# Mean of x block 0 from two partial sums, its statistics later; blocks 1 to 3 normalized in halves; z2 weights in 128-row pieces

## The chip, the cores and the metric

The kernel runs on one core of a Trainium2 chip. A core has five engines that run side by side and meet through semaphores: TensorE (PE; its weight loads are listed as PEld), VectorE (DVE), ScalarE (ACT), GpSimd (POOL) and SyncE (SP, which here only issues DMAs). Sixteen DMA engines move data between device memory and the core's on-chip memory; SP, ACT and POOL each have a queue from which DMAs are issued. TensorE writes to eight banks of PSUM, from which ACT and DVE read.

The metric is the device time of one execution in microseconds. Times inside an execution are counted from the start of its profiled span.

## The reference

With x of 2048 rows (tokens) and 512 columns, all in bf16, the result is a sum of three terms:

```python
xn = layernorm(x)                      # over the 512 columns, eps 1e-5
# A: 32 heads of 16, each token attends to itself and 7 tokens 2, 4, ... 14 back
qkv = xn @ wqkv
attn = softmax(einsum(q, k_gathered) / 4)
a = (attn @ v_gathered) @ wo
# B: gated mixer
z  = gelu(xn @ w_in)                   # 512 -> 1792
z1, z2 = z[:, :896], layernorm(z[:, 896:])
g  = w_sp @ z2 + b_sp[:, None]         # 2048 x 2048, over tokens
b  = (z1 * g) @ w_out
out = x + a + b
```

The change concerns the first microseconds: the layernorm of the first four blocks of 128 tokens, and `z2 = gelu(xn @ w_in[:, 896:])` of these blocks.

## The kernel before

The kernel is one straight program without loops at run time. The 2048 tokens are 16 blocks of 128. Every operation is a task with an engine, what it reads and writes, and an estimated duration (`Plan.add`). A planner (`Plan.schedule`, line 95) puts the tasks of each engine in an order by estimated times. `plan.orders` (line 1053) lists, engine by engine, names of tasks that must follow one another as written, and so fixes nearly all of the order around the change. Each engine then runs its tasks strictly in that order, a DMA issue being a task of the queue's engine. A task waits for the semaphores of what it depends on, and all that stands behind it on the engine waits too.

Layernorm of a block is `ln_block` (line 608): on DVE `bnst` (bn_stats, line 612, sums over 512 columns) and `bnag` (bn_aggr, line 615, mean and variance plus epsilon); on POOL `rstd` (line 617, the power -0.5); on DVE `norm` (line 626, subtract the mean and multiply by rstd). For blocks 0 to 3 TensorE transposes the result by multiplying with a unit matrix (`xTr`, line 642, two halves `a` and `b` of two 128 x 128 tiles each), and ACT copies each half from PSUM to the place of the transposed xn (`xTe`, line 648). Blocks from 4 on are transposed by a DMA (line 630).

Block 0 takes a shorter way, since TensorE has no other work yet. Once the mean is known, x is centred in two halves (`ctr1`, `ctr0`, line 621) and transposed without rstd; z2 of this block is computed from the centred x, and rstd is applied as the scale of the gelu that reads PSUM (`z2g0`, line 829). The properly normalized block 0, needed by Q, K, V and z1 later, is made by `norm0` and transposed afterwards in two halves (`xNr0`, `xNr1`, line 661, copied by `xNe`, line 665).

z2 of a block (`z2_block`, line 806) is two halves of 448 columns (`z2_b_0`, `z2_b_1`), each four matmuls (line 818) that add up over the four 128-row chunks of the weights, and a gelu with its sum. For blocks 0 to 3 each half is two tasks of two matmuls, `a` for chunks 0 and 1 and `b` for 2 and 3. The weights of a half come in two loads of 256 rows (`ld_win_h`, line 555): chunks 2 and 3 on the ACT queue, 0 and 1 on SP's. Four such loads (`ldw_in2a_0`, `ldw_in2a_1`, `ldw_in2b_0`, `ldw_in2b_1`) are issued between the loads of x (`ld_x`, line 545).

Until x arrives TensorE multiplies constants (`warm`, 28 matmuls of 146 columns, line 584), and once more ahead of the first real matmul (`fill0`, 320 columns). Behind the z2 matmuls of blocks 0 to 3 come, without a break in TensorE's order, Q and K (line 694) and V (line 676) of these blocks, then the same for the later ones, z1 (line 841), the token mixing g (line 951) and the outputs (lines 1017 and 1021).

The order of DVE and TensorE in the stretch that the change rewrites:

```python
bnst0 bnag0 ctr1 ctr0 bnst1 bnag1 norm0 norm1 bnst2 bnag2 bnst3 norm2 bnag3 bnst4 norm3
warm xTr0b xTr0a fill0 z2_0_0b z2_0_1b z2_0_0a xTr1a xTr1b z2_0_1a xNr0 z2_1_0a z2_1_0b z2_1_1a xTr2a
xTr2b z2_1_1b xNr1 z2_2_0a z2_2_0b xTr3a xTr3b z2_2_1a z2_2_1b z2_3_0a z2_3_0b z2_3_1a z2_3_1b Q0_0 K0_0
```

Of the kernel before, what the change touches and what calls it, by code (L numbers as in the profile page):

```python
# [14 lines left out]
class Plan:  # L15
# [290 lines left out]
ALU = mybir.AluOpType  # L306
# [9 lines left out]
    warm=28,  # L316
    fill0=1,
# [4 lines left out]
def build_kernel(nc, A_x, A_wqkv, A_wo, B_x, B_w_in, B_w_sp, B_b_sp, B_w_out, out, report=False, sched_kw=None,  # L322
                 cfg=None, emit=True):
    cfg = dict(DEFAULT_CFG, **(cfg or {}))
    S = A_x.shape[1]
# [8 lines left out]
    KP = 16  # L334
    FILL = cfg["fill"]
# [57 lines left out]
    for name, n in (("prime", 4), ("Z", 128), ("st6", NB * 9),  # L393
                    ("mv", NB * 2), ("vpe", NB), ("rstd", NB), ("s1", 2 * NB), ("s2", NB), ("m2", NB), ("msq", NB),
                    ("vpe2", NB), ("rstd2", NB), ("mhalf", 4)):
        foff[name] = fb
        fb += n
# [4 lines left out]
    with ExitStack() as es:  # L402
# [30 lines left out]
        def R1(key, name, n, o_=0):  # L433
            R(key, "sb", [(off[name] + o_, off[name] + o_ + n)])
# [42 lines left out]
        R1("xn0", "attn", 512, 1024)  # L477
        for b in range(NB):
            R(("xnT", b), "sb", [(off["xnT"] + dc * S + 128 * b, off["xnT"] + dc * S + 128 * b + 128)
                                 for dc in range(4)])  # L480
            R1(("OT", b), "OT", 512, 512 * b)
            R1(("z2", b), "z2", FH, FH * b)
        for nm, lo, hi, h0, h1 in (("w_in1", 0, FH, 0, 4), (("w_in2a", 0), FH, FH + HF, 0, 2),
                                   (("w_in2a", 1), FH, FH + HF, 2, 4), (("w_in2b", 0), FH + HF, 2 * FH, 0, 2),
                                   (("w_in2b", 1), FH + HF, 2 * FH, 2, 4)):
            R(nm, "sb", [(off["w_in"] + dc * 1792 + lo, off["w_in"] + dc * 1792 + hi) for dc in range(h0, h1)])
# [66 lines left out]
        def ld_win_h(nm, lo, n):  # L553
            for h in range(2):
                dma(("sp", "act")[h], (lambda h: lambda e: e.dma_start(
                    AC(off["w_in"] + lo + 2 * 1792 * h, [[1792, 2], [1, n]]),
                    B_w_in[256 * h: 256 * h + 256, lo: lo + n].rearrange("(c p) n -> p c n", p=128)))(h),
                    256 * n * 2, (nm, h), writes=[(nm, h)], name="ld%s_%d" % (nm, h))
# [3 lines left out]
        ld_win_h("w_in2a", FH, HF)  # L562
        ld_win_h("w_in2b", FH + HF, HF)
        ld_x(2, "act")
        ld_x(3, "sp")
        for which, eng in ((0, "sp"), (1, "sp")):
            dma(eng, (lambda which: lambda e: e.dma_start(
                AC(off["wqk"] + 512 * which, [[1024, 4], [1, 512]]),
                A_wqkv[:, 512 * which: 512 * which + 512].rearrange("(c p) n -> p c n", p=128)))(which),
                512 * 512 * 2, ("wqk", which), reads=[("w_in2b", 1)],  # L570
                writes=[(("wq", "wk")[which], c) for c in range(4)],
                name="ld%s" % ("qk"[which]))
        for b in range(4, min(8, NB)):
            ld_x(b, "sp", after=[("w_in2b", 1)])
# [33 lines left out]
        def ln_block(b):  # L608
# [10 lines left out]
            if b == 0:  # L619
                for h in (1, 0):  # L620
                    T("dve", (lambda h: lambda v: v.tensor_scalar(A("attn", 256, 256 * h), xin[:, 256 * h: 256 * h + 256],  # L621
                                                                  Fv("mv", 1, 2 * b), None, ALU.subtract))(h),
                      reads=[("xin", xs_), ("mv", b)], writes=[("xc", h)], est=250, name="ctr%d" % h)
            xo = off["attn"] + 1024 if b == 0 else off["xn"] + 512 * sl
            xk = "xn0" if b == 0 else ("xn", sl)
            T("dve", lambda v: v.tensor_scalar(AC(xo, [[1, 512]]), xin, Fv("mv", 1, 2 * b),
                                               Fv("rstd", 1, b), ALU.subtract, ALU.mult),
              reads=[("xin", xs_), ("mv", b), ("rstd", b)], writes=[xk], est=400, name="norm%d" % b)
# [6 lines left out]
            src, sk = (off["attn"], lambda h: ("xc", h)) if b == 0 else (xo, lambda h: xk)  # L635
# [19 lines left out]
        def xn0_half(h):  # L655
            k = next_bank()

            def tr(t):
                last = None
                for i in range(2):  # L660
                    last = t.matmul(ps[:, 512 * k + 128 * i: 512 * k + 128 * i + 128],  # L661
                                    A("attn", 128, 1024 + 256 * h + 128 * i), ident, start=True, stop=True)
                return last
            T("pe", tr, reads=["xn0", "ident"], writes=[("ps", k)], est=2 * c_mm(128), name="xNr%d" % h)
            T("act", lambda a: a.activation(AC(off["xnT"] + 2 * h * S, [[S, 2], [1, 128]]),
                                            ps[:, 512 * k: 512 * k + 256].rearrange("p (c n) -> p c n", c=2), ACTF.Copy),
              reads=[("ps", k)], writes=[("xnTh", 0, h)], est=c_act(256) - 30, name="xNe%d" % h)
# [138 lines left out]
        def z2_block(b):  # L806
            for hf in range(2):
# [5 lines left out]
                def mm(t, hs, first, k=k, c0=c0):  # L813
                    last = None
                    for h in hs:
                        for dc in (2 * h, 2 * h + 1):
                            st = AC(off["attn"] + 512 + 128 * dc if b == 0 else off["xnT"] + dc * S + 128 * b, [[1, 128]])
                            last = t.matmul(ps[:, 512 * k: 512 * k + HF], st, AC(off["w_in"] + 1792 * dc + c0, [[1, HF]]),  # L818
                                            start=(h == first and dc == 2 * h), stop=(h != first and dc == 2 * h + 1))
                    return last  # L820
                if b < 4:
                    for n_, h in enumerate((1, 0) if b == 0 else (0, 1)):
                        T("pe", (lambda mm, h: lambda t: mm(t, (h,), 1 if b == 0 else 0))(mm, h),
                          reads=[("xcT", h) if b == 0 else ("xnTh", b, h), (wk_, h)], writes=[("ps", k)], est=2 * c_mm(HF),
                          name="z2_%d_%d%s" % (b, hf, "ab"[h]))
                else:
                    T("pe", (lambda mm: lambda t: mm(t, (0, 1), 0))(mm), reads=[("xnT", b), (wk_, 0), (wk_, 1)],
                      writes=[("ps", k)], est=4 * c_mm(HF), name="z2_%d_%d" % (b, hf))
# [55 lines left out]
        for j in range(NJ):  # L884
# [6 lines left out]
            if j == 0:  # L891
                for fn_, b, k0 in ((ln_block, 0, 3), (xn0_half, 0, 3), (ln_block, 1, 1), (z2_block, 0, 5), (ln_block, 2, 3),
                                   (z2_block, 1, 7), (xn0_half, 1, 5), (ln_block, 3, 5), (z2_block, 2, 1), (z2_block, 3, 3)):
                    ring[0] = k0
                    fn_(b)
                setup_masks()
                ring[0] = 5
            else:
                for b in bl:
                    ln_block(b)  # L900
# [149 lines left out]
        for q in qord:  # L1050
# [4 lines left out]
                bnst0 bnag0 ctr1 ctr0 bnst1 bnag1 norm0 norm1 bnst2 bnag2 bnst3 norm2 bnag3 bnst4 norm3  # L1055
            """.split(),
            """
                actprime ldw_in2a_1 ldw_in2b_1 ldx2 xTe0b xTe0a xTe1a xTe1b xNe0 z2g0_0 z2g0_1 xTe2a xTe2b xNe1 z2g1_0
                xTe3a xTe3b z2g1_1
            """.split(),  # L1060
            """
                ldx0 ldx1 ldw_in2a_0 ldw_in2b_0 ldx3 ldx4 ldx5 ldq ldk ldx6 ldx7 ldwv
            """.split(),
            """
                warm xTr0b xTr0a fill0 z2_0_0b z2_0_1b z2_0_0a xTr1a xTr1b z2_0_1a xNr0 z2_1_0a z2_1_0b z2_1_1a xTr2a
                xTr2b z2_1_1b xNr1 z2_2_0a z2_2_0b xTr3a xTr3b z2_2_1a z2_2_1b z2_3_0a z2_3_0b z2_3_1a z2_3_1b Q0_0 K0_0
                Q0_1 K0_1 Q0_2 K0_2 Q0_3 K0_3 V0 V1 V2 V3 V4 V5 V6 V7 Q1_0 K1_0 Q1_1 K1_1 Q1_2 K1_2 Q1_3 K1_3 z2_4_0
                z2_4_1 z2_5_0 z2_5_1 z2_6_0 z2_6_1 z2_7_0 z2_7_1 V8 V9 V10 V11 Q2_0 K2_0 Q2_1 K2_1 Q2_2 K2_2 Q2_3 K2_3
                z2_8_0 z2_8_1 z2_9_0 z2_9_1 z2_10_0 z2_10_1 z2_11_0 z2_11_1 V12 V13 V14 V15 Q3_0 K3_0 Q3_1 K3_1 Q3_2
                K3_2 Q3_3 K3_3 z2_12_0 z2_12_1 z2_13_0 z2_13_1 z2_14_0 z2_14_1 z2_15_0 z2_15_1 z1_0_0 z1_1_0 z1_2_0  # L1070
                z1_3_0 z1_4_0 z1_5_0 z1_6_0 z1_0_1 z1_1_1 z1_2_1 z1_3_1 z1_4_1 z1_5_1 z1_6_1 z1_0_2 z1_1_2 z1_2_2 z1_3_2
                z1_4_2 z1_5_2 z1_6_2 z1_0_3 z1_1_3 z1_2_3 z1_3_3 z1_4_3 z1_5_3 z1_6_3 g0_0 g1_0 g2_0 g3_0 g4_0 g5_0 g6_0
                g0_1 g1_1 g2_1 g3_1 g4_1 g5_1 g6_1 g0_2 g1_2 out0_0 out2_0 g2_2 g3_2 g4_2 g5_2 out1_0 out3_0 g6_2 out4_0
                out6_0 g0_3 g1_3 out5_0 out7_0 g2_3 g3_3 g4_3 g5_3 g6_3 out8_0 out10_0 out9_0 out11_0 out12_0 out14_0
                out13_0 out15_0 out15_1 out15_2
# [93 lines left out]
```

## Time and profile before

| what | value |
|---|---|
| median of three runs | 235.44 us (235.41 to 235.62) |
| the profiled execution | 235.56 us, its span 233.7 us |
| TensorE matmuls busy | 229.1 us (98%) |
| DVE / ACT / POOL busy | 202.5 / 119.2 / 51.3 us |
| x block 0 landed, first work of DVE on it | 3.13 us |
| first z2 matmul | 5.27 us |
| first Q matmul | 12.97 us |
| end of the last matmul in the chain | 231.44 us |

The profile of an execution gives each instruction with its engine, its start and duration, the source line (L818 is line 818 of the kernel), the tiles it writes and reads, and how long its engine was idle just before it, with what ended that wait. Matmuls are pipelined, so a record's length (0.35 us for 448 columns) is more than the time from one start to the next. The chain that ended last is followed back from the last instruction, at each step to what released it, or to the instruction before it on its engine: it is the list of what set the time.

### The profile page before, as it was taken

The numbers are of one execution on the slowest core, as the hardware profiler recorded it, in microseconds if no ns is written. First come the engines' busy times: TensorE is split into PE (matmuls) and PEld (weight loads), VectorE is DVE, ScalarE is ACT, GpSimd is POOL, SyncE is SP. The second block draws the span as 40 slices with busy tenths as digits, with TensorE's granted clock in tenths as the row PEclk, the third lists the DMA queues.
The fourth block names the chain that finished last, engine by engine and source line by source line (L and its number), as shares of the span: only waits on it lengthen the run. The fifth ranks groups of instructions, "written<-read, shape, count | busy, mean of one in ns | idle before, by whom it ended". The sixth has DMA issues, their size and how long they took to land.

```text
span 233.7 us, 2996 instructions
## 1 busy us (share of the span) xinstructions
PE 229.1 (98%) x1108; PEld 112.6 (48%) x1127; DVE 202.5 (87%) x231; ACT 119.2 (51%) x235; POOL 51.3 (22%) x67
## 2 busy tenths in 40 slices
PE   7999999999999999999999999999999999999996
PEld 6554455554554444444444444444444444444444
DVE  4779979989989989998999999999999999989200
ACT  3898678989988978952021124342232415101442
POOL 4528965680880050001301000010000000000000
DMA  7897850399909999681429999999939694920412
GB/s 230 270 246 172 188 137 3 109 198 334 357 22 175 227 253 242 125 227 57 139 74 282 244 178 262 185 279 306 295 73 267 128 235 122 237 39 7 112 48 67
DMA packets 87166, 41.76 MB, mean 179 GB/s; under 512 B 66272, under 2 KB 86000, under 8 KB 87152
## 3 DMA queue, kind: packets, MB, share of 16 engines
q1 hardware_dynamic: 71072, 23.24, 48.2%
q10 hardware_dynamic: 14640, 14.13, 21.0%
q0 software_dynamic: 1440, 4.21, 5.9%
q8 instruction: 9, 0.15, 0.3%
q14 instruction: 5, 0.04, 0.1%
HBM read 20.05 MB, written 5.26 MB: 108 GB/s over the span
## 4 chain that ended last, share of the span: by engine, by line
PE 96%; DMA 1%; issue 1%; DVE 1%; ACT 0%
PE ps L951 41%; PE ps L694 12%; PE ps L818 11%; PE ps L1021 10%; PE ps L841 10%; PE ps L1017 6%; PE ps L676 6%; DMA arena<-in_A_x_dram 1%; PE ps L642 1%; DVE fpool L612 0%; ACT arena L648 0%; DVE arena L621 0%; ACT arena L1030 0%; PE ps L661 0%; DVE fpool L615 0%
## 5 line engine op out<-in xcount | busy, mean ns | idle before, releaser
L951 PE MATMUL ps<-arena 128*128 128x512 bf16 x440 | 97.1, 379 | 0.4
L951 PEld LDWEIGHTS ps<-arena 128*128 128x128 bf16 x448 | 43.8, 98 | 52.8
L945 ACT ACTIVATE ps<-arena 128x512 f32<-128x512 bf16 x28 | 16.5, 599 | 47.8 <-DVE arena L958 47.1
L976 DVE TENSOR_TENSOR arena<-arena 128x4096 bf16<-128x4096 bf16 x16 | 36.3, 2284 | 0.3
L718 DVE TENSOR_TENSOR arena<-arena 128x4096 bf16<-128x4096 bf16 x16 | 36.1, 2280 | 0.1
L980 DVE TENSOR_TENSOR arena<-arena 128x4096 bf16<-128x4096 bf16 (+1 forms) x16 | 28.0, 1753 | 0.3
L694 PE MATMUL ps<-arena 128*128 128x512 bf16 x127 | 28.1, 379 | 0.1
L723 DVE TENSOR_TENSOR arena<-arena 128x4096 bf16<-128x4096 bf16 x12 | 27.4, 2287 | 0.2
L1021 PE MATMUL ps<-arena 128*128 128x512 bf16 (+2 forms) x123 | 26.8, 355 | 0.2
L818 PE MATMUL ps<-arena 128*128 128x448 bf16 x128 | 25.7, 353 | 0.2 <-ACT arena L648 0.2
L1030 ACT ACTIVATE arena<-ps 128x512 bf16<-128x512 f32 (+2 forms) x17 | 9.6, 562 | 30.3 <-PE ps L1021 30.3
L841 PE MATMUL ps<-arena 128*128 128x512 bf16 x109 | 24.0, 379 | 0.2
L694 PEld LDWEIGHTS ps<-arena 128*128 128x128 bf16 x128 | 14.5, 113 | 13.1
L958 DVE TENSOR_TENSOR arena<-ps,arena 128x512 bf16<-128x512 f32 x28 | 19.1, 681 | 1.3 <-PE ps L951 1.3
L1021 PEld LDWEIGHTS ps<-arena 128*128 128x128 bf16 x126 | 13.6, 113 | 11.0
L702 ACT ACTIVATE arena<-ps 128x1024 bf16<-128x1024 f32 x16 | 16.3, 1020 | 3.4 <-PE ps L694 3.0
L818 PEld LDWEIGHTS ps<-arena 128*128 128x128 bf16 x128 | 12.1, 98 | 11.4 <-ACT arena L648 1.0
L846 ACT ACTIVATE arena<-ps 128x512 bf16<-128x512 f32 x28 | 16.0, 595 | 3.2 <-PE ps L841 2.7
L829 ACT ACTIVATE arena<-ps 128x448 bf16<-128x448 f32 x30 | 16.2, 548 | 2.2 <-issue 0.2
L841 PEld LDWEIGHTS ps<-arena 128*128 128x128 bf16 x112 | 11.0, 98 | 13.1
L1017 PE MATMUL ps<-arena 128*128 128x512 bf16 (+2 forms) x71 | 16.7, 355 | 0.1
L851 ACT ACTIVATE arena<-arena 128x896 bf16<-128x896 bf16 x16 | 15.1, 943 | 0.1
(65 smaller groups left out, 194.7 us busy)
## 6 DMA issues: line engine op xcount, KB each, us to landing
arena<-vscr ACTq DMA_DIRECT2D x8, 1152.0 KB, 9.7
arena<-in_A_x_dram ACTq DMA_DIRECT2D x17, 128.0 KB, 5.8
vscr<-arena POOLq DMA_DIRECT2D x16, 128.0 KB, 2.4
arena<-in_A_x_dram SPq DMA_DIRECT2D x15, 128.0 KB, 2.9
out_dram<-arena ACTq DMA_DIRECT2D x15, 128.0 KB, 1.9
arena<-in_A_wqkv_dram SPq DMA_DIRECT2D x3, 512.0 KB, 5.8
ascr<-arena POOLq DMA_DIRECT2D x4, 256.0 KB, 5.1
arena<-ascr POOLq DMA_DIRECT2D x4, 256.0 KB, 4.3
```

The source lines that it names most:

```text
L694: last = t.matmul(bank(k + which), AC(off["wqk"] + 1024 * dc + col0, [[4, 128]]), AC(off["xnT"] + dc * S + 512 * j, [[1, 512]]), start=(dc ...
L718: T("dve", lambda v: v.tensor_tensor(pbv, qb, kb, ALU.mult), reads=[("QT", c, j), ("KT", c, j), ("KTpad", c, j)], writes=[("pb", s_)], est ...
L723: T("dve", lambda v: v.tensor_tensor(A("pb", 4096, 4096 * a), A("pb", 4096, 4096 * a), A("pb", 4096, 4096 * b), ALU.add), reads=[("pb", b) ...
L818: last = t.matmul(ps[:, 512 * k: 512 * k + HF], st, AC(off["w_in"] + 1792 * dc + c0, [[1, HF]]), start=(h == first and dc == 2 * h), stop= ...
L841: lastm = t.matmul(bank(k), AC(off["w_in"] + 1792 * dc + 128 * fc, [[1, 128]]), AC(off["xnT"] + dc * S + 512 * j, [[1, 512]]), start=(dc = ...
L945: T("act", lambda a: a.activation(bank(k), A("bbc", 512, 512 * tc), ACTF.Copy), reads=["bbc"], writes=[("ps", k)], est=c_act(512), name="g ...
L951: last = t.matmul(bank(k), AC(off["z2"] + FH * sh + 128 * fc, [[1, 128]]), AC(off["wT"] + WSL * r_ + sh * 512, [[1, 512]]), start=False, s ...
L958: T("dve", lambda v: v.tensor_tensor(uv, bank(k), uv, ALU.mult), reads=[("ps", k)], writes=[("z1T", fc, tc)], est=c_dve(512) + 20, name="u ...
L976: T("dve", (lambda iv, tv, av: lambda v: v.tensor_tensor(tv, iv, av, ALU.mult))(iv, tv, av), reads=[("attn", j), ("Ve", par)], writes=[("V ...
L980: T("dve", (lambda n: lambda v: v.tensor_tensor(AC(off["Vs"], [[4096, 2], [1, n]]), AC(off["Vs"], [[4096, 2], [1, n]]), AC(off["Vs"] + n, ...
L1017: t.matmul(po, AC(off["OT"] + 512 * ot_pos(tb) + 128 * cc, [[1, 128]]), AC(off["wo"] + 512 * cc + c0, [[1, n]]), start=False, stop=False, ...
L1021: last = t.matmul(po, AC(off["z1T"] + fc * S + t0, [[ts, 128]]), AC(off["w_out"] + 512 * fc + c0, [[1, n]]), start=False, stop=(fc == FC - ...
```

## The change

Five things change, all within the first 13 us.

1. The mean of block 0 no longer comes from bn_stats and bn_aggr. ACT sums 192 of the 512 columns (`sxA`, an activation with an accumulator), DVE the other 320 (`sxD`, a tensor_scalar with an accumulator), each scaled by -1/512; `ctr1` and `ctr0` add both sums to x. In ACT's order `sxA` stands behind the DMA issues.
2. bn_stats and bn_aggr of block 0 move behind those of block 1 (`bnst0`) and behind norm1 (`bnag0`); `norm0` moves behind bnag3. The transposes of the normalized block 0 become one task of four (`xNr`), with one copy of 512 columns (`xNe`), and move to just before z2 of block 3.
3. norm1, norm2 and norm3 are two instructions of 256 columns each, and each transposed half needs only its own.
4. The z2 weights come in eight loads of 128 rows instead of four of 256, and z2 of block 0 is eight tasks of one matmul. In TensorE's order these alternate between the two halves and with the transposes of block 1. The loads of Q's and K's weights and of x blocks 4 to 7 wait for the last piece on ACT's queue (`w_in2b`, 3).
5. The constant matmuls are 27 instead of 28.

```diff
-    warm=28,
+    warm=27,
@@
-        def ld_win_h(nm, lo, n):
-            for h in range(2):
-                dma(("sp", "act")[h], (lambda h: lambda e: e.dma_start(
-                    AC(off["w_in"] + lo + 2 * 1792 * h, [[1792, 2], [1, n]]),
-                    B_w_in[256 * h: 256 * h + 256, lo: lo + n].rearrange("(c p) n -> p c n", p=128)))(h),
-                    256 * n * 2, (nm, h), writes=[(nm, h)], name="ld%s_%d" % (nm, h))
+        def ld_win_c(nm, lo, n):
+            for c in (2, 3, 0, 1):
+                dma("act" if c > 1 else "sp", (lambda c: lambda e: e.dma_start(
+                    AC(off["w_in"] + lo + 1792 * c, [[1, n]]), B_w_in[128 * c: 128 * c + 128, lo: lo + n]))(c),
+                    128 * n * 2, (nm, c), writes=[(nm, c)], name="ld%s_%d" % (nm, c))
@@
-                512 * 512 * 2, ("wqk", which), reads=[("w_in2b", 1)],
+                512 * 512 * 2, ("wqk", which), reads=[("w_in2b", 3)],
...
-            ld_x(b, "sp", after=[("w_in2b", 1)])
+            ld_x(b, "sp", after=[("w_in2b", 3)])
@@ ln_block
-            if b == 0:
-                for h in (1, 0):
-                    T("dve", (lambda h: lambda v: v.tensor_scalar(A("attn", 256, 256 * h), xin[:, 256 * h: 256 * h + 256],
-                                                                  Fv("mv", 1, 2 * b), None, ALU.subtract))(h),
...
+            if b in (1, 2, 3):
+                for h in range(2):
+                    T("dve", (lambda h: lambda v: v.tensor_scalar(AC(xo + 256 * h, [[1, 256]]), xin[:, 256 * h: 256 * h + 256],
+                                                                  Fv("mv", 1, 2 * b), Fv("rstd", 1, b), ALU.subtract,
+                                                                  ALU.mult))(h),
...
@@
-        def xn0_half(h):
+        def xn0_T(_):
...
-                for i in range(2):
+                for i in range(4):
...
+        def centre():
+            xin = xin_ap(0)
+            T("act", lambda a: a.activation(A("attn", XA, 1536 + 512 - XA), xin[:, 512 - XA: 512], ACTF.Copy, scale=-1.0 / D,
+                                            accum_out=Fv("sxa", 1)),
+              reads=[("xin", 0)], writes=["xja", "sxa"], est=460, name="sxA")
+            T("dve", lambda v: v.tensor_scalar(A("attn", 512 - XA, 1536), xin[:, 0: 512 - XA], -1.0 / D, None, ALU.mult, ALU.add,
+                                               accum_out=Fv("sxd", 1)),
+              reads=[("xin", 0)], writes=["xjd", "sxd"], est=500, name="sxD")
+            for h in (1, 0):
+                T("dve", (lambda h: lambda v: v.tensor_scalar(A("attn", 256, 256 * h), xin[:, 256 * h: 256 * h + 256],
+                                                              Fv("sxa", 1), Fv("sxd", 1), ALU.add, ALU.add))(h),
+                  reads=[("xin", 0), "sxa", "sxd"], writes=[("xc", h)], est=200, name="ctr%d" % h)
@@ z2_block
+                order = (2, 3, 0, 1) if b == 0 else (0, 1, 2, 3)
+                runs = [(2,), (3,), (0,), (1,)] if b == 0 else [(0, 1), (2, 3)] if b < 4 else [(0, 1, 2, 3)]
...
@@ plan.orders (DVE, ACT, SP, PE)
-                bnst0 bnag0 ctr1 ctr0 bnst1 bnag1 norm0 norm1 bnst2 bnag2 bnst3 norm2 bnag3 bnst4 norm3
+                sxD ctr1 ctr0 bnst1 bnag1 bnst0 norm1a norm1b bnag0 bnst2 bnag2 bnst3 norm2a norm2b bnag3 norm0 bnst4
+                norm3a norm3b bnag4 bnst5 norm4 bnag5 bnst6 norm5 bnag6 bnst7 norm6 bnag7
...
-                actprime ldw_in2a_1 ldw_in2b_1 ldx2 xTe0b xTe0a xTe1a xTe1b xNe0 z2g0_0 z2g0_1 xTe2a xTe2b xNe1 z2g1_0
-                xTe3a xTe3b z2g1_1
+                actprime ldw_in2a_2 ldw_in2a_3 ldw_in2b_2 ldw_in2b_3 ldx2 sxA xTe0b xTe0a xTe1a xTe1b z2g0_0 z2g0_1
+                xTe2a xTe2b z2g1_0 z2g1_1 xTe3a xTe3b xNe z2g2_0 z2g2_1 z2g3_0 z2g3_1
...
-                ldx0 ldx1 ldw_in2a_0 ldw_in2b_0 ldx3 ldx4 ldx5 ldq ldk ldx6 ldx7 ldwv
+                ldx0 ldx1 ldw_in2a_0 ldw_in2a_1 ldw_in2b_0 ldw_in2b_1 ldx3 ldx4 ldx5 ldq ldk ldx6 ldx7 ldwv
...
-                warm xTr0b xTr0a fill0 z2_0_0b z2_0_1b z2_0_0a xTr1a xTr1b z2_0_1a xNr0 z2_1_0a z2_1_0b z2_1_1a xTr2a
-                xTr2b z2_1_1b xNr1 z2_2_0a z2_2_0b xTr3a xTr3b z2_2_1a z2_2_1b z2_3_0a z2_3_0b z2_3_1a z2_3_1b Q0_0 K0_0
...
+                warm xTr0b xTr0a fill0 z2_0_0c2 z2_0_0c3 z2_0_1c2 z2_0_0c0 z2_0_1c3 z2_0_0c1 xTr1a z2_0_1c0 xTr1b
+                z2_0_1c1 z2_1_0a z2_1_0b z2_1_1a xTr2a z2_1_1b xTr2b z2_2_0a z2_2_1a z2_2_0b xTr3a xTr3b z2_2_1b xNr
+                z2_3_0a z2_3_0b z2_3_1a z2_3_1b Q0_0 K0_0 Q0_1 K0_1 Q0_2 K0_2 Q0_3 K0_3 V0 V1 V2 V3 V4 V5 V6 V7 Q1_0
...
```

## The prediction

> **What bounds the kernel now.** I read the page's first part first: TensorE is busy for 98% of the span, every other engine less.
>
> ```profile
> PE 229.1 (98%) x1108; PEld 112.6 (48%) x1127; DVE 202.5 (87%) x231; ACT 119.2 (51%) x235; POOL 51.3 (22%) x67
> ```
>
> So time can be won only where TensorE waits or does useless work. Next the chain that ended last, in order of time (start, duration, what): all that is not TensorE lies before 5.27 us and behind 231.44 us.
>
> ```profile
> 0.73 2.38 DMA arena<-in_A_x_dram
> ...
> 3.13 0.71 DVE fpool L612
> ...
> 3.86 0.21 DVE fpool L615
> ...
> 4.09 0.30 DVE arena L621
> ...
> 4.83 0.39 ACT arena L648
> ...
> 5.27 1.31 PE ps L818 x6
> 6.58 0.04 issue
> 6.62 0.40 PE ps L642 x4
> ...
> 10.42 0.22 PE ps L642 x4
> 10.64 2.27 PE ps L818 x12
> 12.91 0.05 issue
> 12.97 6.85 PE ps L694 x31
> ```
>
> Here the reader sees the head: x block 0 lands, bn_stats and bn_aggr give its mean (3.13 to 4.07), it is centred, transposed, copied, and useful matmuls begin at 5.27. From there to the first Q matmul at 12.97 are 7.70 us. The undisturbed prices are in the chain too: 2.27/12 = 0.189 us per 448-column matmul (L818), 0.22/4 = 0.055 us per transpose. The stage has 32 and 16 of them, 6.93 us; 0.77 us are stalls. The timeline of this stretch shows which (start, busy, what, idle before it):
>
> ```profile
> 2.63 3.69 SPq L545 DMA_DIRECT2D arena<-in_A_x_dram  x3
> ...
> 5.48 0.63 POOL L617 TENSOR_TENSOR fpool<-fpool 128x1 f32<-128x1 f32 x1 [0.66 <-DVE fpool L615]
> ...
> 6.15 0.41 DVE L626 TENSOR_SCALAR arena<-arena,fpool 128x512 bf16<-128x512 bf16 x1 [0.46 <-POOL fpool L617]
> ...
> 6.62 0.23 PEld L642 LDWEIGHTS ps<-arena 128*128 128x128 bf16 x4 [0.48 <-DVE arena L626]
> ...
> 8.06 0.41 DVE L626 TENSOR_SCALAR arena<-arena,fpool 128x512 bf16<-128x512 bf16 x1
> ...
> 9.48 0.11 PEld L818 LDWEIGHTS ps<-arena 128*128 128x128 bf16 x2 [0.17 <-ACT arena L648]
> ```
>
> TensorE waits at 6.62 for norm1, which waited for POOL's rstd1; at 8.62 for norm2; at 9.48 for a copy on ACT. The head of the stage is thus set by one DVE/POOL chain from ctr1 (4.09) on. The x and weight loads are the other input:
>
> ```profile
> DMA to landing us min/median/max: 2.9/4.1/4.4
> ```
>
> That is the four weight loads (L555). The completion records of the trace put them at 3.74, 5.49, 5.67 and 6.55 us, in order of issue and at some 370 GB/s together with the x loads between them.
>
> **The change, part by part.** The sums are made against the profiled execution: span 233.72, its time 235.56, so 1.84 us around the span; the median of the runs, 235.44, is 0.12 lower. I subtract the gain from the median.
>
> *Mean of block 0.* Before, ctr1 starts 0.96 us behind bn_stats (3.13 to 4.09). Now it waits for two sums.
> - sxD on DVE (320 columns and an accumulator): not in the trace. From below, the plain TENSOR_SCALAR of 256 columns, 0.288 (no accumulator); from above, bn_stats with all 512 columns, 0.69, and an accumulator read as ACT's, 0.20: 0.89. It is nearest to bn_stats, which reduces too: L621 and L626 (0.28 and 0.41 for 256 and 512 columns) show a fixed part of 0.15, so 0.15 + 0.54 x 320/512 = 0.49. It ends at 3.13 + 0.49 = 3.62 (3.42 to 4.02).
> - sxA on ACT (192 columns): an L829 of 448 columns takes 0.64 from its start to the end of its accumulator read (11.11 to 11.75); less 256 columns at (565 - 384)/192 = 0.94 ns, 0.40. But ACT stands in order behind its DMA issues, now five instead of three. Three took 0.87 to 2.34, 0.49 each; five end at 3.32. It runs 3.33 to 3.73.
> - ctr1 then starts at 3.77 (0.035 us for a wait, as between DVE's steps) instead of 4.09: 0.32 earlier, set by ACT. Bounds: 3.63 if the issues cost ACT nothing, 4.06 if sxD takes 0.89.
>
> *DVE and POOL behind it.* From ctr1 to norm1 the trace has 2.06 us (4.09 to 6.15): two centrings, bnst1, bnag1, rstd1. The moved bnst0 (0.69) lies in DVE's 0.46 us wait for POOL and the place that norm0 (0.37) had. rstd1 is now POOL's first power; the first one before took 0.68, the second 0.63, so +0.05. norm1a starts at 3.77 + 2.06 + 0.05 = 5.88. The halves start 0.20 apart (as L621's two), last 0.285, so TensorE may transpose from 5.88 + 0.285 + 0.08 = 6.25 instead of 6.62.
> Behind it come norm1b (0.20), bnag0 (0.11), bnst2 (0.72), bnag2 (0.20) and POOL (0.08 + 0.55): norm2a starts at 7.97 and ends at 8.25; before, norm2 ended at 8.47. rstd0 is done by about 7.2, when ACT first needs it for a gelu. norm0, 0.41, goes ahead of bnst4 and norm3a; norm3a ends near 9.75, as norm3 did (9.71), and xTr3a is not before 10.1: covered.
>
> *TensorE.* One filler matmul less (0.12) ends the fillers at 4.15; the first transpose comes 0.43 behind ctr1, at 4.20: nothing on the path. Matmuls of z2_0 start 1.18 behind ctr1 (5.27 - 4.09): 4.95. In the new order: six matmuls to 6.08; xTr1a waits for norm1a, 6.25; then 1c0, xTr1b, 1c1 to 6.85. z2_1_0a needs xTe1a (0.055 + 0.22 + 0.38 + 0.08 behind xTr1a, in the trace 6.62 to 7.38): 6.99. Six matmuls, 8.12; xTr2a waits for norm2a: 8.33, against 8.62. Left from there: 18 matmuls and 12 transposes, 3.40 + 0.66 = 4.06, and a wait of 0.13 for xTe2a ahead of z2_2_0a (it comes 0.73 behind xTr2a, the work between takes 0.60). Q0 begins at 8.33 + 4.06 + 0.13 + 0.05 = 12.57, against 12.97: **0.40 us earlier**.
>
> *Weights in 128-row pieces.* Bytes are equal; four issues more, two on SP, two on ACT. The trace moves one load after the other at about 365 GB/s, so in order of issue the pieces land at 3.4, 4.1, 4.4, 4.7, 5.0, 5.4, 5.7 and 6.4 (the last, with x2 ahead of it), each with up to 0.7 us of one late queue (2b_1: fifteen of sixteen by 4.75, the last 5.49). Needed at 4.95 to 6.66; where one is 0.3 late, xTr2a's wait for norm2a (0.21) takes most. Bounds: 0 to 0.3 lost; I take 0, as xTr2a hides it. On SP, x3 moves from 2.63 to 3.6 and x4 waits for the last ACT piece instead of 2b_1. The wait before ended at 5.51; now at 5.4 to 5.9. Q's and K's weights, behind it, landed at 11.18 and 12.66; at worst 0.4 later, 13.06, ahead of K0_0 at 12.57 + 0.86 = 13.43. x6 has the same delay, and DVE waits for it (13.05): prod0_0 a bit later, with 1.07 us of DVE idle at 31 us to take it.
>
> *xNr and xNe in one.* Four transposes as before; one 512-column copy (0.60, as L846) for two of 0.40: ACT 0.2 less. Hidden.
>
> *Behind 12.97* TensorE never waits (0.05 us pieces of issue alone), and DVE itself waits for TensorE at 120.9, 170.5 and 205.5, so the gain should run through. The last transposed OT lands at 221.2, about 5 us ahead of its use. Sum: 235.44 - 0.40 = 235.04; I say 235.05. Own range: the ctr1 bounds move it by +0.29 and -0.14, late pieces by +0.3, a faster rstd1 by -0.1: 234.75 to 235.4.
>
> **Rivals.** Changes within 0.2% (0.47 us, 234.97 to 235.91) are about what a measurement cannot tell from none.
> 1. *ACT's five issues hold the mean (slower).* Place: sxA. The longest load issue on a queue near here is 0.69 (L575). Five such end at 0.87 + 5 x 0.69 = 4.32, sxA at 4.72, ctr1 at 4.76: 0.67 late, the chain behind it as computed with -0.40 + 0.99: 236.0. It loses once ctr1 passes 4.17. Against: the three issues before took 0.43, 0.48, 0.49.
> 2. *The clock.* 28 fillers of 146 columns take 3.5 us, 0.83 ns a column; L818 has 0.42. The pace thus doubled between 4.0 and 4.5, 3.4 us behind the first filler, though the granted-clock column says 1.00 throughout. If 27 fillers don't bring it about, and another 3.4 us must pass, until 7.6, z2_0 and xTr1 (half pace 3.46 us from 5.2) end at 8.13 instead of 6.85, xTr2a starts at 9.27 instead of 8.33: 235.04 + 0.9 = 235.95. Against: fillers still reach 4.15, and the last filler before (its record is 0.27, not 0.33) suggests a change near 4.15.
>    [...]
> 3. *Pieces land late (no change).* If small loads ran slower or the queue straggled by another 0.7, the last piece lands past 6.66 + 0.35 and each later tenth is lost; with the longest landing before (4.4 from an issue at 3.06) it is 7.46, so 0.45 lost: 235.5. Against: 128 KB x loads between 224 KB ones did not lower the rate.
>    [...]
> 4. *The stalls close as well.* If ACT issues in no time (ctr1 3.63) and rstd takes 0.55, xTr2a comes 0.25 earlier and the 0.13 wait shrinks: 234.65.
>
> **How the numbers follow.** Forecast 0.60, rival 1 0.10, rival 2 0.08, rival 3 0.13, rival 4 0.09. The forecast's own range has somewhat under half below 234.97 (0.25), the rest within 0.2%. Faster: 0.25 + 0.09 = 0.34. Slower: rival 2, most of rival 1, a corner of rival 3: 0.17. Same: 0.49. The range 234.6 to 235.7 leaves out rival 2 and the upper part of rival 1, about 0.17.
>
> **What would show it.** Right: ctr1 near 3.77 with ACT's sum as releaser, z2 from 4.95, xTr2a held by norm2a near 8.3, Q0 near 12.57, nothing changed behind it. Wrong: fast-paced L818 rows missing before 7 us (rival 2), LDWEIGHTS of L818 released by in_B_w_in loads (rival 3), ACT's sum past 4.1 (rival 1), or a new TensorE gap behind 12.97.

## The result, and the profile after

The changed kernel takes 236.96 us (median of six runs, 236.35 to 237.29), the kernel before on the same chip 235.53 us (six runs, 235.41 to 235.66): a ratio of 1.0059, 95% interval 1.0046 to 1.0072. It is slower by 1.4 us; the prediction said 0.4 us faster and gave slower 0.17. The profiled execution of after is its fastest, 236.35 us with a span of 234.35.

The chain that ended last, from x2's issue to the first transposes of block 2 (start, duration, what):

```profile
2.72 4.42 DMA arena<-in_A_x_dram
7.13 0.02 issue
7.16 0.70 DVE fpool L616
7.86 0.02 issue
7.88 0.21 DVE fpool L619
8.09 0.07 issue
8.16 0.56 POOL fpool L621
8.72 0.03 issue
8.74 0.36 DVE arena L627
9.10 0.05 issue
9.15 0.29 PE ps L648 x2
```

Before, this chain was TensorE's own from 5.27 us on. Now it is a load until 7.13: x2, issued by ACT behind four weight pieces at 2.72, lands at 7.13 (before 5.92), and block 2's statistics, rstd and first half norm follow one after the other, so that xTr2a starts at 9.15. Before, it started at 8.62; the forecast was 8.33.

The timeline of the same stretch (start, busy, what, idle before it and its releaser):

```profile
2.98 0.49 DVE L680 TENSOR_SCALAR_CACHE_REDUCE arena<-arena 128x320 bf16<-128x320 bf16 x1 [1.65 <-DMA arena<-in_A_x_dram]
3.22 0.36 ACT L677 ACTIVATE arena<-arena 128x192 bf16<-128x192 bf16 x1 [0.98 <-DMA arena<-in_A_x_dram]
...
3.79 0.60 DVE L684 TENSOR_SCALAR arena<-arena,fpool 128x256 bf16<-128x256 bf16 x2 [0.30 <-ACT arena L677]
...
5.22 1.91 PE L837 MATMUL ps<-arena 128*128 128x448 bf16 x6
...
5.93 0.17 PEld L837 LDWEIGHTS ps<-arena 128*128 128x128 bf16 x2 [0.61 <-DMA arena<-in_B_w_in_dram]
...
6.58 0.11 PEld L837 LDWEIGHTS ps<-arena 128*128 128x128 bf16 x2 [0.48 <-DMA arena<-in_B_w_in_dram]
...
7.16 0.69 DVE L616 BATCH_NORM_STATS2 fpool<-arena 128x6 f32<-128x512 bf16 x1 [0.53 <-DMA arena<-in_A_x_dram]
```

The mean came as forecast: ctr1 starts at 3.79, released by ACT's sum. The first z2 matmul starts at 5.22, where 4.95 was forecast and 5.27 was measured before. Behind it TensorE's weight loads wait twice for pieces of w_in, 1.1 us together. What the core's transfers did shows in the table by stretch (stretch, length, busy time and count of each engine, granted clock, DMA share, GB/s). Before:

```profile
3.20:4.00 0.80, 0.80 (x9) 0.80 (x7) 0.77 (x2) 0.00 (x0) 0.00 (x0) 1.00 1.07 370
4.00:4.80 0.80, 0.55 (x8) 0.33 (x6) 0.77 (x4) 0.00 (x0) 0.66 (x1) 1.00 1.09 372
4.80:5.60 0.80, 0.58 (x5) 0.18 (x3) 0.77 (x3) 0.66 (x2) 0.14 (x2) 1.00 1.08 370
```

and after:

```profile
3.20:4.00 0.80, 0.80 (x9) 0.71 (x6) 0.49 (x3) 0.46 (x2) 0.00 (x0) 1.00 0.79 192
4.00:4.80 0.80, 0.73 (x7) 0.40 (x5) 0.80 (x3) 0.11 (x1) 0.00 (x0) 1.00 0.86 249
4.80:5.60 0.80, 0.71 (x4) 0.14 (x2) 0.77 (x3) 0.55 (x2) 0.30 (x1) 1.00 1.03 338
```

The last column is the reading: 370 GB/s became 192 and 249. By the completion records the pieces land at 3.22, 4.37, 5.70, 5.89, 6.35, 6.53, 6.96 and 7.35 us in order of issue, x2 at 7.13 and x3 at 7.66 (before: the four loads at 3.74, 5.49, 5.67, 6.55; x3 6.90).

Q0 starts at 13.39. Against what, needs care: the trace of before lost 19 of its 1127 matmul records, and one of them is Q0's first. Its page's list of groups has both counts (matmuls, then weight loads):

```profile
L694 PE MATMUL ps<-arena 128*128 128x512 bf16 x127 | 28.1, 379 | 0.1
...
L694 PEld LDWEIGHTS ps<-arena 128*128 128x128 bf16 x128 | 14.5, 113 | 13.1
```

The "0.05 issue" before 12.97 in its chain is the seam of that lost record. One matmul of 0.216 earlier, Q0 began at 12.75. So the head lost 13.39 - 12.75 = 0.64 us, and the start of the last matmul of all shows the same (231.84 against 231.20): nothing was won or lost behind Q0.

The rest lies outside the span. Time minus span was 1.84 in the profiled execution of before and is 2.00 in this one; the medians over all runs are 1.80 and 2.11. In the DMA view of the time behind 232 us (queue, kind: packets, MB, share), after has a line that before lacks:

```profile
q14 instruction: 1, 0.01, 0.4%
```

It is one 8 KB load of instructions at 236.1 us, 1.75 us behind the span's end.

### The profile page after: what moved, and what is told of

It reads as the page before. It is cut to its first block, busy times and chain, and to the rows that moved or that the text cites. A ratio compares the mean times of both kernels' runs of the same rounds, so it can differ in the third digit from the quotient of the medians.

```text
span 234.4 us, 3023 instructions
## 1 busy us (share of the span) xinstructions
PE 231.0 (99%) x1126; PEld 112.6 (48%) x1126; DVE 203.3 (87%) x236; ACT 119.6 (51%) x236; POOL 51.1 (22%) x67
## 4 chain that ended last, share of the span: by engine, by line
PE 95%; DMA 2%; ACTq 1%; DVE 1%; ACT 0%; POOL 0%; issue 0%
PE ps L970 41%; PE ps L714 12%; PE ps L1040 10%; PE ps L859 10%; PE ps L837 9%; PE ps L1036 6%; PE ps L696 6%; DMA arena<-in_A_x_dram 2%; ACTq L560 1%; DVE fpool L616 0%; PE ps L648 0%; POOL fpool L621 0%; ACT L594 0%; DVE arena L627 0%; ACT arena L1049 0%
## 5 line engine op out<-in xcount | busy, mean ns | idle before, releaser
L837 PE MATMUL ps<-arena 128*128 128x448 bf16 x128 | 26.5, 356 | 0.1
```

## The experiments

Fourteen kernels ran, in four groups (e1 to e4, e5 to e8, e9 to e11, e12 to e14); each group has its own runs of the kernel before. In the table, span and "around" (time minus span) are medians; the kernel before had spans of 233.8 to 234.0 and 1.80 around.

| run | median us | ratio to before, 95% | span | around |
|---|---|---|---|---|
| after | 236.96 | 1.0059 [1.0046, 1.0072] | 234.85 | 2.11 |
| e1 before, 27 fillers | 235.70 | 1.0005 [0.9991, 1.0018] | 233.85 | 1.80 |
| e2 after, 28 fillers | 236.90 | 1.0053 [1.0037, 1.0069] | 234.70 | 2.14 |
| e3 after, old loads | 236.27 | 1.0026 [1.0017, 1.0036] | 234.00 | 2.30 |
| e4 e3, 28 fillers | 236.23 | 1.0023 [1.0014, 1.0032] | 233.90 | 2.31 |
| e5 before, pieces alone | 236.82 | 1.0052 [1.0036, 1.0068] | 234.75 | 2.06 |
| e6 before, 5 DVE extra | 235.69 | 0.9998 [0.9988, 1.0008] | 233.85 | 1.80 |
| e7 e4, whole norms | 236.09 | 1.0010 [0.9997, 1.0023] | 233.70 | 2.35 |
| e8 after, zero store late | 236.96 | 1.0047 [1.0029, 1.0065] | 234.80 | 2.16 |
| e9 before, 2 ACT extra | 235.81 | 1.0002 [0.9993, 1.0010] | 233.80 | 2.00 |
| e10 e7, two copies on DVE | 235.72 | 1.0004 [0.9994, 1.0013] | 233.70 | 1.99 |
| e11 before, wide loads | 235.99 | 1.0023 [1.0009, 1.0037] | 234.10 | 1.82 |
| e12 e14, wide loads by rows | 236.26 | 1.0026 [1.0017, 1.0035] | 234.10 | 2.10 |
| e13 before, 1 SP wait extra | 235.47 | 1.0000 [0.9991, 1.0010] | 233.60 | 1.86 |
| e14 e10, SP's wait removed | 235.60 | 0.9991 [0.9980, 1.0003] | 233.70 | 1.83 |

**The loads.** Theory: the pieces cost the 1.4 us. Rivals: 27 fillers bring the slow pace; the halves and the new order cost it.

```diff
# e5: the kernel before, only the loads
-  four loads of 256 rows x 448 columns (224 KB)
+  eight loads of 128 rows x 448 columns (112 KB), order and queues as in after
# e3: after, only the loads undone (and z2_0 in pairs of row blocks again)
-  ld_win_c("w_in2a", FH, HF); ld_win_c("w_in2b", FH + HF, HF)
+  ld_win_h("w_in2a", FH, HF); ld_win_h("w_in2b", FH + HF, HF)
# e4: e3, and
-  warm=27,
+  warm=28,
```

> The kernel before with the weights in eight 128-row loads (four issues each on SP and ACT) and nothing else; z2 of block 0 keeps its tasks of two matmuls. Theory P (the small loads leave the DMA engines short of work between 3.2 and 4.4 us, and x block 2 stands two issues later on ACT): last weight piece past 7.3 us, x2 past 7.1, the first Q matmul 0.6 to 1.0 us later, 236.1 to 236.5 us. If the loads were slowed only by what else the change does in these microseconds: 235.5 to 235.8. DVE has as many instructions as before, so by theory T (see the next) no 8 KB instruction load behind the span, time minus span 1.8.

> The changed kernel with the four 256-row weight loads and z2 of block 0 in tasks of two matmuls, as before; mean from two sums, moved statistics, halves and 27 fillers stay. Theory P: x block 2 lands near 5.9 and the last weights near 6.55 again, the head gains, 235.2 to 235.4. Theory C: half pace remains in many executions, 235.8 to 237.

> The changed kernel with 256-row weight loads and 28 fillers: only the mean from two sums, the moved statistics and the halves are left of the change. Both theories: neither late loads nor a late pace, 235.2 to 235.4, executions within 0.3 us. If it is slower than before, a third cause lies in the mean or in the order.

Pieces alone, in the kernel before, raise the span from 234.0 to 234.75; taking them out of after lowers it from 234.85 to 234.0 (e3) and 233.9 (e4). In time none of the three came as forecast: e5 takes 236.82 (236.1 to 236.5 was expected), e3 and e4 take 236.27 and 236.23 (235.2 to 235.4). The spans of e3 and e4 are no shorter than that of before, and their time around the span is 2.3 us. In e5's table by stretch the transfers fall to 139 GB/s:

```profile
4.00:4.80 0.80, 0.64 (x7) 0.38 (x6) 0.77 (x4) 0.00 (x0) 0.68 (x1) 1.00 0.69 139
```

Its chain (start, duration, what) rests on a weight piece until 6.83:

```profile
2.25 4.58 DMA arena<-in_B_w_in_dram
6.83 0.04 issue
6.87 0.93 PE ps L816 x4
```

In e4's table the same stretch moves 340 GB/s:

```profile
4.00:4.80 0.80, 0.80 (x8) 0.43 (x6) 0.80 (x3) 0.12 (x1) 0.00 (x0) 1.00 1.05 340
```

Is it the number of loads (112 KB each), or that a load has one row for each partition? And does POOL's 16 KB store of zeros, which falls into the same time, make the hole?

```diff
# e11: the kernel before; e12: e14 below, with block 0's z2 taken row block by row block
-  w_in2a, w_in2b: two loads each of 256 rows x 448 columns
+  four loads of 128 rows x 896 columns (224 KB, both halves), rows 256 to 511 on ACT, 0 to 255 on SP
# e8: after
-  POOL: zero store, issued at the start
+  POOL: zero store, issued behind rstd3
```

> The kernel before with the z2 weights as four loads of 128 rows by 896 columns (224 KB each, runs of 1792 bytes, two on SP and two on ACT) instead of four of 256 rows by 448 columns; the readers then wait for two pieces in place of one. Theory (a load of 112 KB costs the queues as much as one of 224 KB, so eight of them leave the DMA engines idle): with four loads of 224 KB the rate between 3.2 and 5.2 us is that of before, 340 to 380 GB/s, the last piece lands by 6.6 and x2 by 6.0. Rival (it is the 128 rows, one row for each partition, that are slow): below 250 GB/s there and the last piece behind 7.2, as with the eight. TensorE's first z2 matmuls need two pieces now (landing about 3.7 and 5.5 or 5.7), so 0.1 to 0.4 us more of the span in any case: 235.6 to 236.1 us by the theory, 236.5 or more by the rival.

> The kernel with two sums, whole norms, two copies on VectorE and no wait more on SyncE, and with the z2 weights as four loads of 128 rows by 896 columns, block 0's z2 matmuls taken piece by piece (rows 256 to 383 for both halves, then 384 to 511, then 0 to 127; the transposes of block 1; then 128 to 255). If it is loads of 112 KB that cost, and not pieces as such: pieces land at about 3.7, 5.0, 5.7 and 6.5, TensorE starts z2 at 4.95 and waits at most 0.2 us for them, span 233.4 to 233.7, 235.3 to 235.5 us, ratio 0.998 to 0.9995. If pieces as such cost (more waits, both halves late): waits of 0.5 us and more ahead of z2 matmuls, span 234.1 or more, 235.9 us or more.

> The changed kernel with POOL's 16 KB store of zeros issued behind rstd3 (about 10 us) instead of at 1.7 us. Theory P1 (its packets, at 3.5 to 4.8 us in the changed kernel, block the sixteen engines one after the other and spread the landings of the pieces by up to 1.3 us): last piece by 6.6, 236.2 to 236.5 us. Theory P2 (the hole comes from the small loads themselves, each queue taking some 0.6 us for 128 rows however small): unchanged, last piece 7.3 to 7.8, 236.7 to 237.1.

e11, with 128-row loads of 224 KB, keeps the rate in its table by stretch (the hole in e5's is the 139 GB/s):

```profile
4.00:4.80 0.80, 0.64 (x7) 0.27 (x6) 0.59 (x3) 0.00 (x0) 0.60 (x1) 1.00 0.99 355
4.80:5.60 0.80, 0.56 (x5) 0.25 (x4) 0.74 (x2) 0.66 (x2) 0.07 (x1) 1.00 1.04 364
```

Its pieces land at 3.73, 4.98, 5.67 and 6.45 and x2 at 6.10, close to what the theory had (by 6.6 and by 6.0); TensorE pays 0.45 us at 5.91, where the next z2 group now needs the fourth piece too (span 234.1); that loss was foreseen, at 0.1 to 0.4. e8 keeps its hole (183, 166, 161 and 213 GB/s in the four slices of 0.4 us from 3.2 on) without the store, so the store is not the cause; its last piece lands at 7.98, later than any forecast here. Runs of 896 bytes are not the cause either: the 256-row loads of before have them too.

e12 was a miss. I expected 235.3 to 235.5; it takes 236.26, with a span of 234.1 against e14's 233.7 and 2.10 around it against 1.83. Its loads fell to 278 GB/s between 4.0 and 4.8, and the third and fourth piece landed at 6.27 and 6.82 (e11: 5.67 and 6.45). Its table of waits has one wait of TensorE's weight loads for a piece:

```profile
PEld ps L836 <- DMA arena<-in_B_w_in_dram: 0.4, 1, 0.4
```

But no load stands in its chain; there the first z2 matmuls are slow:

```profile
5.10 1.97 PE ps L836 x6
```

Six at 0.19 would take 1.13 us. The first five of them start 0.34 to 0.37 us apart, the one that waited for its weights among them no later than the others. So this execution lost its time to the pace (below), and that pieces as such cost it is not shown.

Between 3.2 and 4.8 us the four traces with eight loads (after, e2, e5, e8) move 181 to 220 GB/s, the twelve with four loads 322 (e12) to 377. So the split of four loads of 224 KB into eight of 112 KB is the cause shown of the lower rate and of the longer span. Number and size changed together, the bytes being equal, and what in them costs the time is open.

**The clock.**

```diff
# e1: the kernel before;  e2: after, the reverse
-  warm=28,
+  warm=27,
```

> The kernel before with 27 instead of 28 filler matmuls and nothing else. Theory P (the 128-row pieces starve the DMA engines between 3.2 and 4.4 us, so weights and x block 2 land 0.8 to 1.2 us later): no change, 235.5 us. Theory C (27 fillers end just too early to bring TensorE's double pace, which then came at about 5.9 us instead of before 4.5): 0.4 to 1.5 us slower, with executions further apart than 0.3 us, and L818 matmuls 0.37 us apart at the start of z2.

> The changed kernel with 28 fillers again. Theory C: the pace is doubled by 4.5 us again and the executions lie within 0.3 us; what is left is the late loads, 236.1 to 236.4. Theory P alone: as the changed kernel, 236.4 to 237.3.

One filler makes no difference that can be measured, in either kernel: e1's ten executions lie between 235.53 and 236.69 us, the twenty-five of before in its group between 235.37 and 236.41. But the pace itself moves. e2's execution had z2 matmuls 0.19 apart from 5.13 on, and its waits for pieces only grew, as its table of waits has it (us in total, times, longest):

```profile
PEld ps L837 <- DMA arena<-in_B_w_in_dram: 1.6, 2, 1.0
```

After's execution had its first two 0.33 and 0.39 apart, the second of these with a wait for the piece that landed at 5.89, at a granted clock of 1.00 in every row. Of sixteen profiled executions, one each of all kernels here, ten show the first z2 matmuls, behind 5 us, at about half pace (0.29 to 0.39 us apart where 0.19 is the distance later on; four of seven kernels with the mean of before, six of nine with the two sums; 27 and 28 fillers both), until 5.7 to 6.7 us. In e6, on the other hand, the fillers themselves come 0.07 us apart instead of 0.12 from 3.5 us on. So the double pace does not come at one fixed time in these executions. These starts are all that the traces show of it; what sets the pace no run here shows.

**The mean and the halves.**

```diff
# e7: e4, and
-  norm1a norm1b ... norm2a norm2b ... norm3a norm3b    (256 columns each)
+  norm1 ... norm2 ... norm3                             (512 columns)
-  xTr1a z2_0_1a xTr1b
+  xTr1a xTr1b z2_0_1a
```

> The changed kernel with 256-row loads, 28 fillers, norm1 to norm3 whole again and the last two z2 matmuls of block 0 behind both transposes of block 1 as before: mean from two sums, moved statistics and the joined transposes alone. DVE has two instructions more than before instead of five. If the halves cost what the trace of the changed kernel shows (0.26 us between starts, two of them 0.52 against 0.33 for one whole), each norm is 0.19 shorter for DVE: span 0.2 to 0.4 below that with the halves, 233.5 to 233.7. Theory T: whether the late instruction load is there decides on another 0.3: 235.4 without it, 235.8 with it.

e7's span is 233.70, e4's 233.90, the kernel before's 233.9 to 234.0. So two sums and moved statistics gain 0.1 to 0.3 in the span, each against the kernel before in its own group (e7 233.7 against 234.0, e10 233.7 against 233.9, e14 233.7 against 233.8). What e4 has beyond e7, the halves and the order made for them, gives 0.2 of it back. In e4's chain no norm stands, but the last weight load, for which z2_0_1a, now ahead of xTr1b, has to wait:

```profile
2.12 4.68 DMA arena<-in_B_w_in_dram
6.80 0.05 issue
6.85 0.55 PE ps L838 x2
```

So how much of the 0.2 is the halves' own price is not shown. That they have one, the row of after's half norms shows (ns: shortest, median, longest; first and last start):

```profile
L627 DVE TENSOR_SCALAR arena<-arena,fpool x6: 329/339/346, 5.9 to 10.5; 128x256 bf16<-128x256 bf16 x6
```

The nearest row of before, its two centrings, which the prediction went by:

```profile
L621 DVE TENSOR_SCALAR arena<-arena,fpool x2: 281/284/288, 4.1 to 4.3; 128x256 bf16<-128x256 bf16 x2
```

With two operations and two per-partition operands in place of one of each, 256 columns take 0.34 in place of 0.28 and start 0.26 apart, not 0.20 (after's centrings, L684, which add two sums, take 0.34 as well): two halves hold DVE 0.52 where a whole norm takes 0.33 from start to start.

**Outside the span.** Theory: the changed program makes an 8 KB instruction load behind the span, and the time around the span grows. Which engine's program? Only DVE's (e6), only ACT's (e9), only SP's (e13); and ACT's (e10) and then SP's (e14) brought back.

```diff
# e6: before                # e9: before                 # e13: before
+ 5 one-element memsets     + 2 one-element copies       - x4 waits for w_in2b_1
  at DVE's end                on ACT behind ldx2         + x4 waits for w_in2b_1 and w_in2a_1
# e10: e7                                                # e14: e10
- copies of out12_0, out14_0 on ACT                      - x8's load also waits for ACT's sum of block 0
+ copies of out12_0, out14_0 on DVE                      + it waits for DVE alone, whose norm0 comes behind that sum
```

> The kernel before with five one-element memsets on DVE in its idle time at the end, as many instructions as the change adds there, and nothing else. Theory T: the longer DVE program needs one more 8 KB instruction load at the very end, behind the span; time minus span goes from 1.8 to 2.1 to 2.4, the span stays, 235.9 to 236.1 us. Rival (the extra load and the longer tail belong to ACT's or SP's added instructions, or to the order of the head): no change, 235.6 us, no load behind the span.

> The kernel before with two one-element copies more on ACT, behind its x2 issue, where ACT waits for TensorE anyway; nothing else. The theory of the tail (an ACT program longer by some instructions makes one more 8 KB instruction load behind the span's end): span as before, 233.8 to 234.0, time minus span 2.1 to 2.4 instead of 1.80, an instruction load at about 235.9, so 236.0 us, ratio 1.001 to 1.002. Its rival (it is SP's longer program, SP having one wait more in each kernel with the late load): time minus span 1.80, no late load, ratio 1.000.

> Two sums, moved statistics, whole norms, four 256-row loads, 28 fillers (as in the run with whole norms), and the last copies of output blocks 12 and 14 on VectorE instead of ScalarE, so that ACT has one instruction less than in the kernel before, and SP one more. If the tail comes with ACT's count: span 233.7, time minus span 1.80, no late load, 235.5 us, ratio 0.998 to 1.0. If it comes with SP's: time minus span 2.35, 236.05 us, ratio 1.001.

> The kernel before with one wait more on SyncE: x4's load waits for a second weight load, which has landed long before, so nothing moves inside the span. Theory (SyncE's longer program brings time behind the span, beside ScalarE's): span 233.9, time minus span 2.0 or more, 235.9 us. Rival (ScalarE's program alone counts): time minus span 1.80, 235.7 us.

> Two sums, moved statistics, whole norms, 256-row loads, two copies on VectorE, as in the run before it, less the one wait that SyncE had more: the load into block 0's place no longer waits for ScalarE's sum, which the order of the work on VectorE ensures anyway. Theory (SyncE's longer program): span 233.7, time minus span 1.80, 235.5 us, ratio 0.999. Rival (something else in that kernel, such as VectorE's or ScalarE's new program ends): time minus span stays 1.99, 235.7 us.

Five instructions more on DVE leave the time around the span at 1.80 (e6). Two tiny instructions on ACT bring 0.20 (e9) and the late load, with the span unchanged (the whole time, a ratio of 1.0002, does not tell it from none); two copies fewer on ACT take 0.36 off e7; one SP wait brings 0.16 in e10 against e14, while its 0.06 in the kernel before is within the scatter (1.80 to 1.91 in ten of e13's runs, 1.76 to 1.92 in those of before). So small changes to the programs of ACT and, less, of SP move this time, and each expectation that named one engine alone was half right. It does not follow their length: the traces list 313 instructions on ACT and 71 on SP in before (1.80 us around), 314 and 72 in e7 (2.35), 316 and 74 in after (2.11), 310 and 71 in e14 (1.83), 311 and 71 in e12 (2.10). My mechanism, the late load, was not right: the profiled executions of e10 and e12 stand at 2.0 and 2.1 with no late load in the trace, and e11's with a late load was one outlier of 2.34 among runs near 1.82. What the time behind the span is spent on stays open.

e14 is what is left of the change without its costs. Its chain (start, duration, what) is TensorE's own from the fillers on:

```profile
4.33 0.43 PE ps L649 x4
4.76 0.27 PE ps L589
5.02 0.08 issue
5.11 1.72 PE ps L838 x6
6.83 0.22 PE ps L649 x4
7.05 1.67 PE ps L838 x8
```

No wait for a load or for a norm is left, yet it is no measurable gain (0.9991, interval up to 1.0003). TensorE was not free for the earlier mean: ctr1 started at 3.45, the last filler at 4.00, the first transpose at 4.12. And three of those six matmuls took 0.33, 0.37 and 0.29 where the later ones have 0.19 (1.51 for eight at 11.45): 0.42 us, more than the earlier mean won. No version here beats the kernel before by more than the measurement tells.

## Why the prediction was wrong

- **The mean (right up to ctr1, partly by luck).** ctr1 was to start at 3.77, with ACT's sum as releaser: 3.79, released by L677. sxD took 0.49, as sized from bn_stats. Rival 1 (ACT's issues hold the mean) falls at its price: five issues took 0.38 to 0.45 each and ended at 3.17, and the sum started at 3.22. The luck is in x block 0, which landed at 2.96, in before at 3.11. Counted from this landing, ctr1 comes 0.98 later in all seven traces with the old mean, 0.82 in after, where ACT was still issuing, and 0.59 to 0.64 in the six with two sums and three issues on ACT.
- **From ctr1 to z2 (wrong, hidden in the result).** "Matmuls of z2_0 start 1.18 behind ctr1": 1.43 in after, at 5.22 instead of 4.95. The two centrings start 0.26 apart instead of 0.20, and three of the four distances from the first transpose to the filler behind them are 0.11, where before had 0.06. Most of what the mean won was gone before the first useful matmul; the late loads then hid this.
- **The step that failed: "Bounds: 0 to 0.3 lost; I take 0", for the weights in pieces.** The working moved one load after the other at 365 GB/s and put pieces at 3.4 to 6.4; they came at 3.22 to 7.35. The third was due at 4.4 and came at 5.70, and x2, behind four of them on ACT's queue, 1.2 later than before. So norm2 was late and xTr2a started at 9.15, not at 8.33; from there to Q0 it took the 4.24 us that the sum had (4.06 + 0.13 + 0.05). The loss in the span is 0.75 (e5), 0.8 (e2 against e4, both with 28 fillers) or 0.95 (after against e4), two and a half to three times the upper bound. Rival 3 named the mechanism, small loads that run slower, at 0.13, and sized it 0.45 from late weights alone; what it left out is x2 and norm2 behind it, on which the chains of after and e2 rest (those of e5 and e8 rest on a weight piece, until 6.83 and 6.67). The argument against it, "128 KB x loads between 224 KB ones did not lower the rate", was evidence on a mixture, not on a run of eight small ones. In all, the last piece landed at 7.35, 0.8 later than the last of the four loads of before (6.55).
- **The halves (mis-sized).** "The halves start 0.20 apart (as L621's two)": 0.26. L621 has one operation and one per-partition operand (0.28 us), the half norms two of each (0.34 us). norm1a started at 5.92 against 5.88 forecast; behind it each pair costs DVE 0.19 more than a whole norm. e4 against e7: 0.2 in the span, together with the order.
- **The baseline.** Q0 at 12.97 was the second matmul; the true 12.75 makes the stalls of the stage 0.55, not 0.77. Against it the forecast's own Q0, 12.57, is 0.18 earlier and not 0.40: its rows gave 235.26, not 235.04.
- **Rival 2, the clock (half right).** Filler 27 or 28 changes nothing that can be measured (e1 1.0005 to before; e2 236.90 against 236.96). The half pace behind 5 us is real (0.29 to 0.39 us apart in ten of the sixteen traces), comes in 28-filler kernels too, and cost e14's execution 0.42. A slow pace until 7.6, with which the rival's 235.95 was worked out, no trace shows: it lasted until 5.7 to 6.7. The three runs of before, within 0.21 us, were too few to tell whether the start of the double pace moves.
- **What no step had: time outside the span.** The prediction took "1.84 us around the span" as fixed; it is 2.11 for after.

The sum, in medians: mean, statistics and halves together 0 (e4's span is that of before), pieces +0.8 to +0.95, around the span +0.31, together +1.1 to +1.3 of the 1.4 us; the rest is as large as the scatter of the medians of before between the groups (235.53 to 235.76).

## What to carry to other kernels

Price a split of a load by what lands behind it on the same queue, and not at the rate of the larger loads: here eight loads of 112 KB in place of four of 224 KB cost 0.75 us of the span (e5), more than any wait that they could remove. A step that starts useful TensorE work earlier may only move it into a slow pace (here 0.29 to 0.39 us a matmul in place of 0.19, until 6.7 us at the latest), so look at the distance of the first matmuls before counting a gain. Compare time minus span as well as span: here two instructions on ACT moved it by 0.20 us (e9) with the span unchanged, and lost records must be counted before a gap is read.

## What the runs showed that was not expected

- Eight loads of 112 KB on two queues: 181 to 220 GB/s between 3.2 and 4.8 us, where four of 224 KB had 322 to 377.
- x block 0, the first load of all, landing anywhere from 2.70 to 3.38 us in the sixteen traces: about twice what the two sums win at ctr1.
- Time around the span between 1.80 and 2.35 us, moved by a few instructions on ACT and SP that do nothing at the program's end, but not in step with their number; at times with one more 8 KB instruction load (two in e2 and e8), 1.75 us behind the span's end in after.
- A tensor_scalar on DVE of 256 columns: 0.28 us with one operation and one per-partition operand (before, L621), 0.34 with two of each (after, L627 and L684).
- The double pace of TensorE arriving anywhere from 3.5 (e6) to 6.7 us, with a distance of 0.058 between transposes followed by 0.108 and 0.106 in one group (after, from 4.28 on), at a granted clock of 1.00 in the profile's rows.
